# Moving weight conversion, small turning copies and filter loads between VectorE, ScalarE and GpSimd at the start of a kernel for a Fourier filter and a two-layer network

## The chip, the cores and the metric

One NeuronCore of one Trainium2 chip. The metric is device time in microseconds (us) of one execution. Executions of one kernel in one set of rounds lie within 0.33% of each other, and every ratio compares a kernel with runs of the kernel before from the same rounds on the same chip. In the lines of the profile PE is TensorE, PEld its weight loads, DVE VectorE, ACT ScalarE, POOL GpSimd and SP SyncE; a `q` behind the name marks what the engine's queue does besides computing, such as issuing a transfer. The DMA share is the busy share of the 16 DMA engines.

## The reference, cut to what matters

```python
# x: (8, 3008, 256) fp32; filt_r, filt_i: (1505, 256) fp32
X = np.fft.rfft(x, axis=1)
y = np.fft.irfft(X * (filt_r + 1j * filt_i)[None], n=3008, axis=1).astype(np.float32)
# w_in: (256, 2048), w_out: (2048, 256); they arrive as float64
h = y.reshape(8 * 3008, 256) @ w_in
out = ((h - np.tanh(h)) @ w_out).astype(np.float32)
```

The kernel does the transforms as matrix products in two steps (3008 = 47 x 64) through scratch tensors in DRAM, with the filter product between them, and the two large products by a scheme that takes seven block products in place of eight, which needs sums of weight blocks. The weights are doubles, so they are first made fp32 by integer operations on their two 32-bit words.

Words used below. A *piece* is 128x512 doubles (512 KB in DRAM); two pieces make a *quarter*, and there are eight quarters, four of `w_in` and four of `w_out`. The *first stage* is the forward transform of batch 0. The *middle stage* is 16 *steps*; a step is one product `pz`, two filter products on VectorE (`uv`, `zs`), the inverse product `pe`, its copy and its store. Two steps make a *step group*, for which the filter rows are loaded and the matrix `gx` is made ("turned"). The *passage* is what follows up to the main loop. A *unit* is a turn of the main loop, of which there are 192 in all: 14 up products, the shrink, 14 down products. Everything but batch 0's transforms lies in the main loop.

## The kernel before

One piece is converted like this; VectorE and ScalarE share the work, and ScalarE's two steps stand in its queue among its PSUM copies:

```python
def converted(tiles, src, dsts, queue):
    t = tiles("raw", I64, n); queue.dma_start(t, src)                       # cut
    yield
    V.tensor_scalar(out=it, in0=hi, scalar1=0xFFFFF, ..., op0=ALU.bitwise_and)
    ACT.activation(ft, it, AF.Identity, bias=1.0, scale=2.0 ** -20)
    V.tensor_scalar(out=pt, in0=hi, scalar1=20, scalar2=0x7FF, ...)
    ACT.activation(pt, pt, AF.Relu, bias=exp_b)
    V.tensor_scalar(out=st, in0=hi, scalar1=-2 ** 31, ..., op0=ALU.bitwise_and)
    V.scalar_tensor_tensor(out=ft, in0=lo, scalar=2.0 ** -52, in1=ft, ...)
    yield
    V.tensor_scalar_min(pt, pt, 255.0)
    V.scalar_tensor_tensor(out=pt, in0=pt, scalar=23, in1=st, ...)
    for cols, dst, sign in dsts:
        V.scalar_tensor_tensor(out=dst, in0=f, scalar=sign, in1=p, op0=ALU.mult, op1=ALU.mult)
    yield
# after the second piece of a quarter: four sums of 128x256 blocks, G.tensor_sub
```

`V` is VectorE, `ACT` ScalarE, `G` GpSimd. The middle stage and its helpers:

```python
def turned(g3, t):
    ACT.copy(t[0:RP], g3[IM:IM + RP])
    ACT.mul(t[IM:IM + RP], g3[0:RP], -1.0)

def back0():
    ...                                          # two products with mats, two with gx -> pe
    e1 = tr.tile([RP2, 2, DM], F32, tag="e1", bufs=2, name="e1")
    ACT.copy(e1, pe[0:RP2])
    ACT.dma_start(<scratch>, e1)

ws = weights(tiles0, range(5), 2)                # quarters 0 to 4, from the first stage on
for j in range(NK // 2):                         # 16 steps
    c = j // 2
    if j % 2 == 0 and c + 1 < NK // 4:
        a2[c + 1] = load_a2(0, c + 1, False)     # read-back of the first stage
        if c + 2 < NK // 4:
            mats[c + 2] = load_slots(c + 2, pro)
            fts[c + 2] = filters_of(c + 2)       # filter rows, 6 loads issued by GpSimd
    ...                                          # pz, then back0() of the step before
    V.tensor_mul(uv, pz, ft[:, 0])
    V.tensor_mul(zs, pz, ft[:, 1])
    next(ws, None)                               # a half of a piece
    if j % 2 and c + 1 < NK // 4:
        double_filters(fts[c + 1], c + 1)        # two ScalarE copies
        turned(mats[c + 1][1], gx[(c + 1) % 2])
back0(); load_e2(...)
for _ in range(EARLY):                           # EARLY = 3 forward products of the next batches
    next(fs)
```

In the main loop three quarters are left (`weights(tiles1, range(5, 8), 2)`, advanced at k = 0, 2, 4 of a unit), and the filter rows are copied once more for the later batches by small transfers of SyncE's queue.

## Time and profile before

| | us |
|---|---|
| time, median of 3 runs | 2882.33 (2880.47 to 2883.72) |
| same, beside the changed kernel, 6 runs | 2881.78 (2878.38 to 2883.72) |
| first middle product / first filter product | 43.0 / 45.2 |
| last result product ends | 106.6 |
| main loop's first unit starts | 123.4 |
| units 0 to 7 | 138.7 |
| from unit 8 to the end | 2617.2 |

The prediction shows the lines that this rests on. The table is read from the start of each unit's second product and from the first and last records of the step products. The first four rows of times lie in stretches that the change touches; the last, 91% of the time, has the same instructions in both kernels.

### The profile page before, as it was taken

Reading aid. Unit: us, or ns where it says so; the run is one execution under the profiler, and the core shown is the slowest. Engines: PE = TensorE matmul, PEld = TensorE weight load, DVE = VectorE, ACT = ScalarE, POOL = GpSimd, SP = SyncE. Lnnn points to the kernel's source line nnn. Section 1 sums busy time; section 2 is a strip of 40 time slices with the busy share of each in tenths; the row PEclk is TensorE's granted clock in tenths of the full one; section 3 lists DMA queues with packets and bytes.
Section 4 is the critical chain, followed back from the end, with each engine's and each line's share of the span. In section 5 each row is a group of like instructions: output and inputs, shape, how many; then the busy total and the mean of one; then the engine's idle time right before and its main releaser. Section 6 shows DMA issues by size and latency. Waiting matters only on the chain.

```text
span 2879.3 us, 36469 instructions
## 1 busy us (share of the span) xinstructions
PE 2748.1 (95%) x12474; PEld 2278.9 (79%) x12474; DVE 1989.3 (69%) x2214; ACT 1872.2 (65%) x2460; POOL 1743.4 (61%) x1382
## 2 busy tenths in 40 slices
PE   5789999999999999999999999999999999999996
PEld 3467777888878787888877888888888888888885
DVE  4675666766776677766677777766777777777765
ACT  3555666666767676666666676666666676666663
POOL 4345777544677767645576777655476666555544
PEclk7889999999999999999999999999999999999998
DMA  9644443232233332222323233112233222110100
GB/s 270 180 150 116 114 110 91 62 93 81 70 76 84 76 75 53 57 81 83 87 71 75 68 78 81 36 45 67 51 75 81 53 55 56 24 28 16 26 11 16
DMA packets 328061, 217.46 MB, mean 76 GB/s; under 512 B 229085, under 2 KB 280405, under 8 KB 327674
## 3 DMA queue, kind: packets, MB, share of 16 engines
q1 hardware_dynamic: 273176, 160.50, 23.6%
q10 hardware_dynamic: 52738, 51.33, 5.9%
q0 software_dynamic: 1952, 3.22, 0.5%
q8 instruction: 100, 1.64, 0.2%
q14 instruction: 95, 0.78, 0.1%
HBM read 138.81 MB, written 79.17 MB: 76 GB/s over the span
## 4 chain that ended last, share of the span: by engine, by line
PE 69%; DVE 9%; ACT 8%; POOL 5%; issue 4%; DMA 3%; SPq 1%; ACTq 0%; DVEq 0%; POOLq 0%
PE o L590 27%; PE x L483 18%; PE z L483 8%; PE y L483 5%; PE pe L364 3%; PE pu L447 3%; DVE h L544 3%; PE pz L383 3%; ACT y L539 2%; PE pf L304 2%; ACT y L540 1%; POOL t L465 1%; ACT u L489 1%; DVE uv L398 1%; DVE h L519 1%
## 5 line engine op out<-in xcount | busy, mean ns | idle before, releaser
L590 PE MATMUL o<-t,wd 128*128 128x256 f32 (+2 forms) x3072 | 777.9, 376 | 1.8 <-POOL t L464 1.3
L544 DVE TENSOR_TENSOR h<-h,y 128x1024 f32<-128x1024 f32 (+2 forms) x384 | 589.7, 1536 | 256.1 <-ACT y L540 255.9
L462 POOL TENSOR_TENSOR t<-h 128x512 f32<-128x512 f32 (+2 forms) x192 | 240.1, 1250 | 767.5 <-DVE h L548 582.3
L590 PEld LDWEIGHTS o<-t,wd 128*128 128x128 f32 x3072 | 582.0, 191 | 74.4 <-POOL t L464 1.9
L483 PE MATMUL x<-tu,wu 128*128 128x256 f32 (+2 forms) x2304 | 592.2, 380 | 16.5 <-ACT u L489 15.5
L590 PE MATMUL o<-h,wd 128*128 128x256 f32 (+2 forms) x2304 | 581.6, 375 | 0.2 <-DVE h L548 0.2
L548 DVE SCALAR_TENSOR_TENSOR h<-sq,h 128x1024 f32<-128x1024 f32 (+2 forms) x384 | 566.6, 1476 | 20.8 <-ACT y L539 0.5
L483 PEld LDWEIGHTS x<-tu,wu 128*128 128x128 f32 x2304 | 430.2, 191 | 157.2 <-issue 73.2
L590 PEld LDWEIGHTS o<-h,wd 128*128 128x128 f32 x2304 | 431.3, 190 | 70.8 <-issue 18.5
L545 ACT ACTIVATE sq<-y,near_b 128x1024 f32<-128x1024 f32 (+2 forms) x384 | 435.4, 1134 | 5.8 <-DVE h L548 1.1
L539 ACT ACTIVATE y<-h 128x1024 f32<-128x1024 f32 (+2 forms) x384 | 400.0, 1042 | 14.8 <-ACT e L367 6.8
L489 ACT COPY s<-x 128x512 f32<-128x512 f32 (+2 forms) x192 | 110.7, 577 | 458.2 <-PE x L483 449.6
L540 ACT ACTIVATE y<-y 128x1024 f32<-128x1024 f32 (+2 forms) x384 | 399.3, 1040 | 12.2
L465 POOL TENSOR_TENSOR t<-t,h 128x512 f32<-128x512 f32 (+2 forms) x192 | 306.7, 1597 | 0.0
L489 ACT COPY u<-x 128x512 f32<-128x512 f32 (+2 forms) x384 | 219.2, 571 | 73.0 <-PE x L483 35.5
L399 POOL TENSOR_TENSOR zs<-zs,ft 128x512 f32<-128x512 f32 x112 | 166.3, 1485 | 142.3 <-ACT zs L397 142.2
L463 POOL TENSOR_TENSOR t<-h,t 128x512 f32<-128x512 f32 (+2 forms) x192 | 241.6, 1258 | 15.0
L464 POOL TENSOR_TENSOR t<-h 128x512 f32<-128x512 f32 (+2 forms) x192 | 249.5, 1300 | 0.0
L400 POOL TENSOR_TENSOR uv<-uv,zs 128x512 f32<-128x512 f32 x112 | 211.3, 1887 | 16.0 <-DVE uv L398 7.8
L483 PE MATMUL x<-ut,wu 128*128 128x256 f32 (+2 forms) x768 | 200.0, 383 | 12.2 <-DVE h L519 10.7
L483 PE MATMUL z<-tu,wu 128*128 128x256 f32 (+2 forms) x768 | 195.4, 377 | 0.5 <-DVE h L525 0.5
L483 PE MATMUL z<-ut,wu 128*128 128x256 f32 (+2 forms) x768 | 194.8, 376 | 0.0
(113 smaller groups left out, 3236.6 us busy)
## 6 DMA issues: line engine op xcount, KB each, us to landing
a<-ct SPq DMA_DIRECT2D x64, 384.0 KB
ct<-e ACTq DMA_DIRECT2D x128, 192.0 KB
ft<-filt SPq DMA_DIRECT2D x96, 256.0 KB
out_dram<-ot SPq DMA_DIRECT2D x1408, 16.0 KB
ct<-a ACTq DMA_DIRECT2D x80, 256.0 KB
x_sb<-in_x_dram SPq DMA_DIRECT2D x69, 256.0 KB
e<-ct SPq DMA_DIRECT2D x33, 512.0 KB
fg<-fg SPq DMA_DIRECT2D x40, 392.0 KB
```

The lines of the kernel that those rows point to most:

```text
L462: G.tensor_sub(t[0], b[0][1], b[0][0])
L463: G.tensor_sub(t[1], b[1][1], t[0])
L464: G.tensor_sub(t[2], b[1][1], b[0][1])
L465: G.tensor_sub(t[3], t[1], b[1][0])
L483: nc.tensor.matmul(bank[:, k], wu[:, q - 1, (2 * u + k) * 128:(2 * u + k + 1) * 128], rhs[q - 1], start=(first and k == 0), stop=True, ski ...
L489: ACT.copy(t, X)
L539: ACT.activation(y[k], ht[k], AF.Arctan, scale=S)
L540: ACT.activation(y[k], y[k], AF.Square)
L544: V.tensor_mul(ht[k], ht[k], y[k])
L545: ACT.activation(sq[k], y[k], AF.Square, bias=near_b, scale=A)
L548: V.scalar_tensor_tensor(out=ht[k], in0=sq[k], scalar=K, in1=ht[k], op0=ALU.add, op1=ALU.mult)
L590: nc.tensor.matmul(product(q), wd[:, q - 1, (2 * u + k) * 128: (2 * u + k + 1) * 128], rhs[q - 1][:, k], start=(u == 0 and k == 0 and q == ...
```

## The change

Its intent: free ScalarE from weight conversion in the first stage, so that its PSUM copies follow TensorE; let VectorE do three quarters alone there and start the middle stage with fewer pieces left; take waits for buffers out of the middle steps (four result buffers instead of two, read-backs two groups ahead); take the passage's third forward product away; and leave two quarters instead of three to the main loop, in single steps instead of blocks, with the filter copies made few and large on GpSimd. The diff, cut to its core:

```diff
-EARLY = 3
+EARLY = 2
 def converted(...):
+        if alone:
+            V.tensor_scalar(out=ft, in0=it, scalar1=2.0 ** -20, scalar2=1.0, op0=ALU.mult, op1=ALU.add)
+            V.tensor_scalar(out=pt, in0=pt, scalar1=-896.0, scalar2=0.0, op0=ALU.add, op1=ALU.max)
+        else:
+            ACT.activation(ft, it, AF.Identity, bias=1.0, scale=2.0 ** -20)
+            ACT.activation(pt, pt, AF.Relu, bias=exp_b)
 ... (one manual_schedule region around everything, where there were two)
 def turned(g3, t):
-    ACT.copy(t[0:RP], g3[IM:IM + RP])
-    ACT.mul(t[IM:IM + RP], g3[0:RP], -1.0)
+    G.tensor_copy(t[0:RP], g3[IM:IM + RP])
+    G.tensor_scalar_mul(t[IM:IM + RP], g3[0:RP], -1.0)
-ws = weights(tiles0, range(5), 2)
+ws = weights_alone(tiles0, range(3))             # first stage, all of it ahead of the steps
+ws = weights(tiles0, range(3, 6), 2)             # middle stage, a piece finished one call later
-    e1 = tr.tile([RP2, 2, DM], F32, tag="e1", bufs=2, name="e1")
+    e1 = e1s[0:RP2, j % 4]
-        a2[c + 1] = load_a2(0, c + 1, False)
+        if c + 2 < NK // 4:
+            a2[c + 2] = load_a2(0, c + 2, False, ("a2", "ft")[c % 2])
 ... (main loop)
-    for c in range(NK // 4):
-        filters_of(c, filt_d)                    # 52 copies on SyncE
+    for v, row, m, i, n, src in filter_rows(0, NK):
+        G.dma_start(<filt_d>, src)               # 10 copies on GpSimd
-late = weights(tiles1, range(5, 8), 2)
+late = weights_slow(tiles1, range(6, 8))
-    if k in (0, 2, 4):
-        next(late, None)
-    elif U > 0:
-        next(copies, None)
+    next(late, None)
+    if U > 0 and k in (1, 3):
+        next(copies, None)
```

## The prediction

> **What bounds the kernel now.** I read the page first, then busy time by stretch, then the chain of waits of the first 125 us, then the waits. The page's slices of 72 us each show TensorE busy from the third slice to the end, and the DMA engines busy only at the start:
>
> ```profile
> PE   5789999999999999999999999999999999999996
> ...
> DMA  9644443232233332222323233112233222110100
> ```
>
> I compared the instruction order of both kernels on every engine. Apart from names they are the same from about the eighth unit of the main loop on (3175 of 3332 listed rows on PE, 2666 of 2862 on DVE), so only the time before that can change. A unit is a quarter of a group of four rows: 14 up products, the shrink, 14 down products; there are 192. From the start of each unit's second product I cut the beginning in four: first stage (forward transforms of batch 0, 0 to 43), middle stage (16 steps, to 107), passage to the main loop (to 123.4), units 0 to 7 (to 262.1). The view of busy time by stretch:
>
> ```profile
> 0.00:43.00 43.00, 14.63 (x26) 5.30 (x27) 12.05 (x26) 14.59 (x24) 18.56 (x33) 0.79 0.95 280
> 43.00:107.00 64.00, 52.87 (x194) 36.01 (x195) 47.92 (x90) 38.34 (x57) 33.94 (x56) 0.88 0.86 219
> 107.00:123.40 16.40, 8.99 (x26) 5.74 (x25) 0.83 (x1) 3.51 (x6) 1.44 (x3) 0.70 0.50 150
> 123.40:262.10 138.70, 118.92 (x469) 91.27 (x468) 97.01 (x124) 80.83 (x108) 53.98 (x51) 0.91 0.47 141
> 262.10:2879.00 2616.90, 2552.65 (x11763) 2140.56 (x11762) 1831.48 (x1975) 1734.92 (x2265) 1635.45 (x1243) 1.00 0.27 65
> ```
>
> Columns: stretch, length, PE, PEld, DVE, ACT, POOL busy, granted clock, DMA share, GB/s. The last row, 91% of the time, has PE at 98% and does not change. The 262 us before it hold the whole prize. The first stage is full on DMA (0.95), the middle stage nearly so (0.86); neither is full on any engine. The chain of waits there:
>
> ```profile
> 5.59 15.56 DMA raw<-in_moe_w_in_dram
> ...
> 21.80 0.63 ACT conv L205
> ...
> 58.71 4.96 DMA filt<-in_filt_i_dram
> 63.67 0.53 ACT filt L840
> ...
> 110.93 3.30 DMA x_sb<-in_x_dram
> ...
> 114.36 2.06 PE pf L304 x2
> ```
>
> First, ScalarE's half of a weight conversion stands ahead of PSUM copies in its queue and waits for weights that land at 21.15. Then the middle stage waits for filter rows. Then the first unit waits for an input tile queued behind a load that waits. The waits of 0 to 120 us (total, times, longest):
>
> ```profile
> ACT e L901 <- DMA ct<-e: 11.4, 5, 5.5
> ...
> DVE uv L922 <- ACT filt L839: 6.7, 3, 3.7
> ```
>
> The waits of SyncE's queue in the same stretch:
>
> ```profile
> SPq L417 <- DMA ct<-e: 19.6, 2, 11.0
> ```
>
> The waits of 123 to 262 us, where PE stands for a ScalarE copy that frees its bank and for input tiles:
>
> ```profile
> PE x L483 <- ACT u L489: 12.4, 5, 3.8
> ...
> PE pf L304 <- DMA x_sb<-in_x_dram: 6.9, 3, 4.2
> ```
>
> [...] three queues run and the share is 0.95. [...] the copies at 22.94 wait behind the conversion at 21.80. [...] Here single-source conversion steps start 0.34 us apart, two-tensor ones 0.61 to 0.73. [...] the three writes of a converted piece (L222) take 0.83 us alone and 3.92 us at 152.85 and at 192.27, in the combining sums of GpSimd.
>
> **The change part by part.**
>
> First stage. Before, two loads of late weights (1.05 MB) belong to the second region and yet stand sixth in SyncE's order, at 15.15; one region puts them after the first tiles of the main loop. That takes 1.05 MB at 280 GB/s, 3.7 us, out of a full stage. ScalarE loses its conversions, so its PSUM copies follow PE, which had all inputs but PSUM space at 19.4. Now the last copy is at 33.46, the stores issue to 35.1, the read-back issues at 38.31 and the first middle product starts at 43.02. I expect that product at 35 to 37. But six pieces, not three, stand on VectorE ahead of its first middle product, without help. One piece: three masks 1.02, two more single-source steps 0.68, then 0.61, 0.46, 0.73, 0.68: 4.2 us. Six from about 20.5 are 25 us, with 2 to 3 us for slowing by GpSimd's sums: about 48, where the first filter product now is at 45.16. So the 7 us do not reach VectorE; it starts about 3 us later.
>
> Middle stage. VectorE has 16 x 2 products at 0.60, 19.2 us, and six pieces at about 3.7, 22: 41 us, now 47.9 busy (seven pieces). Four result buffers instead of two take away "ACT e <- DMA ct<-e" (11.4 us; two waits, 5.5 and 3.5, stand ahead of the doubling of filters). Four a2 buffers load read-backs two steps ahead. ScalarE loses 8 x 1.03 us of turning, which GpSimd takes. A conversion is now finished one call later, so VectorE doesn't stand for ScalarE. If VectorE starts at 48, works 41 and waits 10 of the present 16, it ends at 99, now 104. By DMA: 219 GB/s x 64 us is 14.0 MB, plus the 1.05 MB moved here is 15 MB; from 36, at 246 GB/s (the rate of 40 to 80 us), that is 61 us: 97. Both say the stage ends at 99 to 100 instead of 107. Gain 7 us.
>
> Passage. EARLY = 2 takes away the third forward product, whose input stands behind a SyncE wait of 11 us and costs PE 6.05 us just ahead of the first unit. The path that stays is last store, second part of the tile, its products, two copies: about 12 us for 16.4. Gain 4 us.
>
> Units 0 to 7. Four late pieces for six: 2 x 6.3 us less VectorE time (a piece averages 6.3 us here: 2.8, 4.1, 3.6, 5.2, 3.0, 6.4 and 12.6 us over the six are 37.7). They are cut in five calls per unit, not run as blocks between the additions that free PSUM. 60 filter copies leave SyncE's queue for 10 large ones on GpSimd's, so input tiles no longer stand behind them (6.9 us of PE waits, of which I take 5). One more forward product costs 0.9. PE has 118.9 us of work at clock 0.91; 19.8 us are idle. I take 10 us of idle away, and 5 to 6 us of busy time because a steadier PE was granted more in this trace (1.00 in the stretches without holes, 0.72 in the one with most). 138.7 becomes about 123.5. Gain 15 us.
>
> Sum: 7 + 4 + 15 = 26 us, so 2882.3 - 26 = 2856 us.
>
> **The rivals.**
> 1. DMA is the bound of everything up to the main loop, and the order doesn't matter. For: 0.95, 0.86, and the same bytes but for their place. Against: in slices of 20 us the share falls to 0.76 (80 to 100) and 0.56 (100 to 120). Then the beginning gives at most 3 us, units 15: about 2864.
> 2. The conversions on VectorE become a new wait: six pieces in a row delay the middle stage, and GpSimd's sums of quarter 2 stand ahead of the filter rows of step group 2, which now are issued near 51 and land near 60 by a latency of 7 to 8 us. [...] Against: group 2 starts only at 63.66 today. If it holds, the beginning loses 3 to 5 us: about 2870.
> 3. PE fills the first units wholly and the start is DMA-tight at 0.98: 262 us x the idle I see allows 10 + 5 us at the start and 25 in the units: about 2840. Against: unit 1 has no down products, and the shrink's chain bounds it.
> 4. The large filter copies on GpSimd delay its combining sums (t), which three of the four down groups need. A GpSimd issue takes 0.54 us with 24, 28 or 64 runs alike, so I expect 10 x about 1 us off the path; if a copy of 496 runs costs several us each, 10 us of the gain go: 2866.
>
> **Range and chances.** The steps add to 26 us with 7 (start) and 7 (units) of doubt, and the rivals span 2840 to 2870. Eight in ten: 2838 to 2873. Over 2% needs 58 us of 262, more than PE idle and DMA slack I can name (about 40): 0.04. Slower by 2%: 0.01. Within: 0.95.
>
> **What would show it.** Right: first middle product before 38, first filter product near 48; last result copy near 98; first unit near 112; units 0 to 7 in 120 to 127 us; from unit 8 on 2617 us as before. Wrong: the middle stage still ending after 104 (rival 1 or 2: DMA share 0.95 says 1, gaps on DVE after the sums say 2); units 1 to 4 still over 18 us with VectorE full; a GpSimd issue over 2 us (rival 4); or the late part changing by more than 5 us, which would break the premise.

## The result, and the profile after

The changed kernel takes 2871.68 us (median of 6, 2866.68 to 2872.49) against 2881.78 us. The ratio is 0.9963, 95% interval 0.995 to 0.9975. A ratio here is the mean time of one kernel's runs over that of the other's runs of the same rounds, so it is not quite the ratio of the medians quoted. So the gain is 10 to 11 us, where 26 were predicted. It is clear of the noise and inside the stated range, but by the 2% rule the verdict is "same".

Where it came from needs more than one trace of each kernel, because single traces of one kernel differ in the table below by 0.4 us (first middle product) to 5.6 us (from unit 8 on). There are three of each (the two first profiles, and the runs `after_again`, `after_b`, `before_b`, `before_c` below):

| us, three traces and their mean | before | after | difference | predicted |
|---|---|---|---|---|
| first middle product starts | 43.0, 43.0, 42.6: 42.9 | 41.8, 42.2, 41.7: 41.9 | -1.0 | 35 to 37, so -6 to -8 |
| first filter product starts | 45.2, 45.2, 44.7: 45.0 | 52.1, 51.8, 51.7: 51.9 | +6.9 | +3 |
| last result product ends | 106.6, 108.8, 105.3: 106.9 | 115.0, 113.6, 113.9: 114.1 | +7.2 | -7 |
| passage (from there to the first unit) | 16.8, 16.6, 16.2: 16.5 | 12.7, 13.5, 13.6: 13.3 | -3.2 | -4 |
| units 0 to 7 | 138.7, 136.7, 134.0: 136.5 | 120.4, 119.1, 119.1: 119.5 | -16.9 | -15 |
| from unit 8 on | 2617.2, 2621.8, 2621.6: 2620.2 | 2616.3, 2621.9, 2621.6: 2619.9 | -0.3 | 0 |

The last four rows add up to -13.2 us in the traces; the timed difference is 10.7 (0.0037 of 2881.8), and single executions of either kernel spread over some 5 us. The gains of the passage and of units 0 to 7 came as forecast; the time up to the last result product, forecast to shrink by 7, grew by 7.

Busy time by stretch of the changed kernel, cut at the same events as the five lines of the kernel before (columns as there: stretch, length, PE, PEld, DVE, ACT, POOL busy with counts, granted clock, DMA share, GB/s):

```profile
0.00:41.80 41.80, 13.66 (x26) 4.96 (x27) 19.84 (x44) 10.06 (x16) 20.78 (x34) 0.83 0.91 258
41.80:114.80 73.00, 54.32 (x192) 38.58 (x193) 56.21 (x103) 30.17 (x41) 52.04 (x75) 0.77 0.82 210
114.80:127.70 12.90, 7.56 (x26) 5.60 (x25) 0.82 (x1) 2.92 (x5) 1.50 (x3) 0.69 0.82 244
127.70:248.10 120.40, 112.85 (x472) 88.00 (x471) 81.87 (x106) 78.87 (x105) 58.85 (x56) 0.96 0.52 155
248.10:2864.40 2616.30, 2552.98 (x11763) 2138.55 (x11761) 1828.85 (x1975) 1734.85 (x2265) 1637.03 (x1243) 1.00 0.26 65
```

Read row by row. First: ScalarE's work fell from 14.6 to 10.1 us as intended, the DMA rate fell from 280 to 258 GB/s, and the stretch is only 1.2 us shorter. Second: ScalarE fell from 38.3 to 30.2, VectorE rose from 47.9 to 56.2 and GpSimd from 33.9 to 52.0, and the stretch grew by 9 us. Fourth: TensorE is 94% busy where it was 86%; its idle time fell from 19.8 to 7.5 us, its busy time from 118.9 to 112.9 at a granted clock of 0.96 instead of 0.91. Fifth: the same work.

The waits of 0 to 125 us (total, times, longest), which answer to the two of the kernel before that the prediction shows:

```profile
ACT e1s L951 <- PE pe L948: 44.7, 10, 19.7
...
DVE uv L972 <- ACT filt L878: 10.4, 5, 5.5
...
PEld pe L948 <- POOL gx L888: 6.3, 1, 6.3
...
PE pe L948 <- POOL gx L888: 5.9, 1, 5.9
```

The wait of ScalarE's result copies for their stores (11.4 us before) is gone, as forecast. The wait of VectorE for doubled filters grew from 6.7 to 10.4. And a wait stands here that the kernel before had only in shares of 1 us: the inverse product stands 5.9 us for `gx`, now made by GpSimd. The chain of waits passes through it:

```profile
97.76 0.73 POOL wd L260
...
99.37 1.15 POOL wd L262
100.52 0.86 POOL wd L263
101.44 0.85 POOL gx L887
102.37 1.25 POOL gx L888
103.66 1.17 PE pe L948 x2
```

The timeline of GpSimd just before (start, length, engine, line, operation; in brackets the idle time and what ended it) shows why `gx` came so late:

```profile
88.37 0.60 POOL L874 DMA_DIRECT2D filt<-in_filt_r_dram  x1
88.96 0.55 POOL L874 DMA_DIRECT2D filt<-in_filt_i_dram  x1
91.23 0.58 POOL L874 DMA_DIRECT2D filt<-in_filt_r_dram  x1 [1.71 <-DMA filt<-in_filt_r_dram]
93.30 0.54 POOL L874 DMA_DIRECT2D filt<-in_filt_i_dram  x1 [1.49 <-DMA filt<-in_filt_i_dram]
```

GpSimd's instructions stand in this trace in the order of the program: ten issues for the filter rows of the last step group (steps 14 and 15), two of them waiting for transfers, then the four sums of a quarter of `w_out`, and only then the turning for the group before (steps 12 and 13): 15 us from 88.4 to 103.6, of which the turning itself is 2. The effect on the steps: up to the filter products of step 12 (96.4 us, against 95.9 before) the changed kernel had made up nearly all of its late start; step 14 then begins at 108.8 instead of 101.9.

In units 0 to 7 TensorE's wait for a ScalarE copy that frees its bank has shrunk from 12.4 us, and a line for input tiles, 6.9 us before, is no longer there:

```profile
PE x L547 <- ACT u L553: 7.1, 4, 4.9
```

### The profile page after: what moved, and what is told of

Same layout as the page of the kernel before. It is cut to its first block, busy times and chain, and to the rows that moved or that the text cites.

```text
span 2864.4 us, 36448 instructions
## 1 busy us (share of the span) xinstructions
PE 2741.4 (96%) x12474; PEld 2275.7 (79%) x12474; DVE 1987.6 (69%) x2226; ACT 1856.9 (65%) x2432; POOL 1770.2 (62%) x1408
## 4 chain that ended last, share of the span: by engine, by line
PE 71%; DVE 9%; ACT 8%; POOL 5%; issue 4%; DMA 2%; ACTq 0%; SPq 0%; DVEq 0%; POOLq 0%
PE o L654 28%; PE x L547 18%; PE z L547 8%; PE y L547 5%; PE pe L411 3%; PE pu L511 3%; PE pz L430 3%; DVE h L608 3%; ACT y L603 2%; PE pf L351 2%; ACT y L604 1%; POOL t L529 1%; ACT u L553 1%; DVE uv L445 1%; DVE h L583 1%
## 5 line engine op out<-in xcount | busy, mean ns | idle before, releaser
L547 PE MATMUL x<-tu,wu 128*128 128x256 f32 (+2 forms) x2304 | 589.0, 378 | 11.1 <-ACT u L553 10.1
L654 PEld LDWEIGHTS o<-h,wd 128*128 128x128 f32 x2304 | 430.8, 190 | 71.1 <-issue 18.3
L603 ACT ACTIVATE y<-h 128x1024 f32<-128x1024 f32 (+2 forms) x384 | 400.0, 1042 | 15.1 <-ACT e L414 7.5
L527 POOL TENSOR_TENSOR t<-h,t 128x512 f32<-128x512 f32 (+2 forms) x192 | 241.2, 1256 | 15.1
L563 DVE TENSOR_TENSOR h<-y,s 128x512 f32<-128x512 f32 (+2 forms) x192 | 130.3, 678 | 94.9 <-PE y L547 86.9
L547 PE MATMUL y<-ut,wu 128*128 128x256 f32 (+2 forms) x768 | 194.6, 376 | 0.0
```

What stands on the lines that cost most here:

```text
L527: G.tensor_sub(t[1], b[1][1], t[0])
L547: nc.tensor.matmul(bank[:, k], wu[:, q - 1, (2 * u + k) * 128:(2 * u + k + 1) * 128], rhs[q - 1], start=(first and k == 0), stop=True, ski ...
L603: ACT.activation(y[k], ht[k], AF.Arctan, scale=S)
L654: nc.tensor.matmul(product(q), wd[:, q - 1, (2 * u + k) * 128: (2 * u + k + 1) * 128], rhs[q - 1][:, k], start=(u == 0 and k == 0 and q == ...
```

## The experiments

All edits are to the changed kernel unless another is named. Times are medians of 4 or 5 runs (single runs in part D), ratios against the kernel before. "First unit" and "last product" are the start of the main loop's first unit and the end of the last result product in the profiled execution.

### A. The turning, and the middle stage

**after_again**: the changed kernel once more.

> The changed kernel once more, as a control for its own spread. Expected: ratio to before 0.995 to 0.998 again. Its beginning should show the same parts as in the first trace: first filter product near 52, a wait of about 6 us of PE for the turned matrices of GpSimd near 98 to 104, first unit near 127.7, units 0 to 7 in about 120 us, 2616 us from unit 8 on. If the first unit starts later than 130 in this trace, the spread of the changed kernel's times (2867 to 2872) lies in the beginning.

2870.68 us, 0.9963 [0.9949, 0.9976]. The result stands.

**t_act**: the turning back on ScalarE.

```diff
-    G.tensor_copy(t[0:RP], g3[IM:IM + RP])
-    G.tensor_scalar_mul(t[IM:IM + RP], g3[0:RP], -1.0)
+    ACT.copy(t[0:RP], g3[IM:IM + RP])
+    ACT.mul(t[IM:IM + RP], g3[0:RP], -1.0)
```

> The changed kernel with the turning of the matrices back on ScalarE. Theory (GpSimd's queue is the new wait: turning stands behind filter row issues, their waits, and sums): the 5.9 us wait of PE for gx goes, the filter rows are issued earlier, the middle stage ends 5 to 8 us sooner and the first unit starts at 120 to 123; total 5 to 8 us under the changed kernel, ratio to before 0.993 to 0.995. Rival (the stage's DMA bytes set its end): the wait moves to the filter rows or read-backs of the last group, the first unit stays at 126 or later, ratio 0.996.

2868.27 us, 0.9946 [0.9933, 0.996]; last product 112.3, first unit 125.5, 2 us sooner than the changed kernel's mean. A part of the loss only, and in the time not resolved from the changed kernel (0.9963 [0.9949, 0.9976]). TensorE's longest wait for `gx` in this trace is 0.6 us, so taking that wait away by this road is not enough: ScalarE is busy 19.4 us in 75 to 107 us where it was 13.6.

**t_first**: the turning stays on GpSimd, but is issued half a group sooner, ahead of the filter rows of the next group and of the sums.

```diff
-    (at odd j)  double_filters(fts[c + 1], c + 1); turned(mats[c + 1][1], gx[(c + 1) % 2])
+    (at even j, after back0)  turned(mats[c + 1][1], gx[(c + 1) % 2]); fts[c + 2] = filters_of(c + 2)
+    (at odd j)  double_filters(fts[c + 1], c + 1)
```

> The changed kernel with turning still on GpSimd, but issued ahead of the filter rows of the group after next, so that no sum and no filter issue stands between. It tells the place in the queue from the work. Theory of the queue: the gx wait of 5.9 us goes, gain 3 to 6 us on the changed kernel (ratio 0.994 to 0.996). If turning on GpSimd costs by its work or by slowing VectorE, this is no better than the changed kernel (0.9963).

2860.72 us, 0.9927 [0.9913, 0.994]: 10 us better than the changed kernel, intervals apart. GpSimd's timeline of this kernel for the same turning, now ahead of the last filter rows:

```profile
90.98 0.50 POOL L887 COPY gx<-fg 48x384 f32<-48x384 f32 x1 [2.43 <-DMA fg<-fg]
91.56 1.19 POOL L888 TENSOR_SCALAR gx<-fg 48x384 f32<-48x384 f32 x1
...
93.23 0.60 POOL L874 DMA_DIRECT2D filt<-in_filt_r_dram  x1
```

The long wait for `gx` is gone; its longest left in this trace is 0.9 us. Last product 110.0, first unit 124.0, where the changed kernel has 114.1 and 127.4. So the order in GpSimd's queue was a cost of the change, and about the whole loss against the kernel before (123.4). Its trace accounts for 3.4 us at the first unit, not for all 10 that the timing shows; the profiled execution was the slowest of its five (2866.14). What the other 6 are is not found; the part from unit 8 on took 2619.6 us in this trace, and it varies by 5 us from trace to trace in kernels that are alike there (part D).

That only brings the beginning back to where it was; the forecast wanted it 11 us sooner. The next runs ask what holds it then.

**no_loads** (wrong): t_first, with pieces 6 to 11 converted from the raw tiles of pieces 3 to 5 instead of being loaded, so 3.1 MB fewer are moved in the middle stage and VectorE's work stays.

```diff
+    (pieces 6 to 11)  t = loaded[3 + len(loaded) % 3]     # no transfer
```

> On the kernel t_first, pieces 6 to 11 of the weights (the six converted during the middle stage) are converted from pieces 3 to 5, already in SBUF, so six loads of 0.52 MB are not made; all instructions of the engines stay. The result is wrong on purpose. Theory (the middle stage's end is set by DMA bytes): 3.1 MB at the 229 GB/s of 75 to 107 us are 13.7 us, so the first unit starts 9 to 14 us sooner than in t_first (124.0), at 110 to 115. Rival (engine queues set it, VectorE's row of conversions and GpSimd's queue): under 4 us, first unit at 120 or later.

Last product 106.4, first unit 119.1: 4.9 us sooner than t_first. Time 2860.07, 0.993 [0.9915, 0.9945], no different from t_first's. The 4.9 us lie between the theory (9 to 14) and its rival (under 4). Busy time in 75 to 107 us, of t_first and of no_loads:

```profile
75.00:107.00 32.00, 24.34 (x97) 17.07 (x98) 26.61 (x51) 16.33 (x22) 26.37 (x40) 0.95 0.90 229
```

```profile
75.00:107.00 32.00, 27.31 (x114) 18.60 (x115) 28.22 (x52) 18.27 (x26) 29.13 (x42) 1.00 0.59 168
```

The DMA share falls from 0.90 to 0.59, and VectorE and GpSimd are then busy 28.2 and 29.1 of 32 us. The bytes were a limit, and another stands right behind it.

**alone2**: t_first, with two quarters converted by VectorE alone before the steps instead of three, and the third with ScalarE's help among the steps.

```diff
-ws = weights_alone(tiles0, range(3))
+ws = weights_alone(tiles0, range(2))
-ws = weights(tiles0, range(3, 6), 2)
+ws = weights(tiles0, range(2, 6), 2)
+    (at j % 4 == 3)  next(ws, None)              # one more call, so that it ends in time
```

> On t_first, only two quarters instead of three are converted by VectorE ahead of the middle stage, the third with the rest during it (four extra calls). Theory (DMA sets the stage's end, so when VectorE starts doesn't matter): first filter product at 42 to 45 instead of 51.9, yet the first unit still at 122 to 126, total within 3 us of t_first (2860.7). Rival (the six pieces in a row cost the stage what they delay it): first unit 4 to 8 us sooner, ratio to before 0.990 to 0.9915.

The first filter product comes at 41.3 instead of 51.9, and the last product still ends at 108.4; 2860.64 us, 0.993 [0.9917, 0.9944], the same as t_first. Ten us of earlier start bought less than two at the end: the six pieces in a row ahead of the first step cost little, because the same work only moved behind it. Two things in this trace are easily overlooked. The first middle product comes at 39.1, sooner than in any trace of the changed kernel (taken up in the part on the prediction's first stage). And in 42 to 75 us the DMA engines are full, with a share of 1.05 where t_first has 0.88:

```profile
42.00:75.00 33.00, 24.91 (x99) 17.57 (x97) 24.83 (x46) 15.94 (x23) 27.16 (x40) 0.93 1.05 263
```

**alone2_no_loads** (wrong): alone2 without the loads of pieces 6 to 11.

> alone2 and no_loads together: VectorE starts the middle stage at 41 instead of 52, and six of the weights' loads are not made. The result is wrong on purpose. Theory (two limits side by side: bytes hold the stage to 108 to 110, VectorE's work after a start at 52 holds it to 106; each alone gave 2 to 5 us): with both lifted the last product of the stage ends at 94 to 99 and the first unit starts at 106 to 112, 8 us or more before either alone (119.1, 120.8). Rival (a third limit, the chain of filter rows, ScalarE's doubling and VectorE): first unit stays at 116 or later.

Last product 108.2, first unit 119.8; 2859.04 us, 0.9927 [0.9912, 0.9942]. With the DMA share at 0.46 in 75 to 107 us the stage ends where it did; the expectation's rival came true, not its theory.

**alone2_light** and **alone2_light_no_loads** (both wrong): alone2 with pieces 6 to 11 not converted, their places filled with zeros by VectorE (ScalarE's two steps per piece go too); the first still loads them, the second doesn't. With the two runs above that makes all four combinations.

```diff
+    if 6 < len(loaded) <= 12:                    # pieces 6 to 11
+        for cols, dst, sign in dsts:
+            V.memset(dst, 0.0)
+        return
```

> Kernel alone2 (two quarters converted by VectorE alone, GpSimd turning ahead of its filter rows), with pieces 6 to 11 still loaded but not converted: their places are filled with zeros by two or three memsets on VectorE (wrong on purpose). About 6 x 5 us of VectorE's work in the middle stage goes, the bytes stay. If VectorE's conversions are the limit of the middle stage: last result product at 98 to 102 instead of 108.4, first unit near 111 to 115 instead of 120.8. If the DMA engines' bytes are: 106 to 109 and 119 to 121, no change, DMA share 0.9 in 75 to 107 us. If neither alone (both side by side, each hiding the other): 104 to 107. Rest unchanged but for the zeros; read the first unit's start, not the total.

> As alone2_light, and pieces 6 to 11 not loaded either (wrong on purpose): both the bytes (3.1 MB) and VectorE's conversions of the middle stage go. If these two are the whole limit: last result product at 88 to 95, first unit at 100 to 107. If the chain of the 16 steps itself (filter rows, GpSimd's queue, ScalarE's copies and result stores) is a third limit close behind: last result product still at 100 to 106, with VectorE busy under 20 of 32 us in 75 to 107 and DMA share under 0.6.

| last product ends / first unit starts, us | six pieces converted | not converted |
|---|---|---|
| six pieces loaded | 108.4 / 120.8 | 105.2 / 118.0 |
| not loaded | 108.2 / 119.8 | 100.8 / 113.2 |

Busy time in 75 to 107 us, of alone2, alone2_no_loads, alone2_light and alone2_light_no_loads in this order:

```profile
75.00:107.00 32.00, 23.61 (x83) 16.46 (x84) 29.14 (x54) 16.51 (x23) 23.84 (x36) 0.84 0.74 209
```

```profile
75.00:107.00 32.00, 26.04 (x89) 17.79 (x88) 28.91 (x54) 16.38 (x23) 26.23 (x36) 0.79 0.46 122
```

```profile
75.00:107.00 32.00, 24.98 (x92) 16.70 (x92) 12.56 (x28) 13.77 (x18) 22.28 (x35) 0.84 0.80 213
```

```profile
75.00:107.00 32.00, 24.49 (x90) 16.70 (x90) 10.79 (x26) 11.77 (x16) 21.10 (x34) 0.89 0.57 161
```

Taking away the bytes alone gives 0.2 us at the last product, the conversions alone 3.2, both 7.6. These are single traces, and three traces of one kernel differ by 1.4 us (changed) to 3.5 us (before) at this event. What is firm is that both together give far more than either. Which of the two comes first is less sure; the traces suggest VectorE's conversions (29 of 32 us busy), with the bytes close behind them (without the conversions, VectorE waits 24.5 us in 42 to 107 us for filters that ScalarE doubles, and ScalarE in turn 13.0 for the filter rows to land), and the 99 to 100 us of the forecast are all but reached only with both gone. The expectation for the second run, 88 to 95, was too hopeful: with VectorE busy for a third of 75 to 107 us and the DMA engines for 0.57 of it, the steps end at 100.8, within the 100 to 106 of that expectation's alternative. That this is the chain of the 16 steps itself is not shown: in 42 to 75 us the DMA share is 1.01 to 1.05 in all four kernels, so the transfers that are left fill that stretch. The zeros are no help in the late part: 2619.3 and 2616.6 us from unit 8 on, within the spread seen above. The totals, 2860.59 (0.9925 [0.9906, 0.9945]) and 2853.37 us (0.9905 [0.9888, 0.9921]), against 2860.64 for alone2 and 2859.04 for alone2_no_loads, say the same: one gone gives nothing that is resolved, both gone 7 us (its interval just touches alone2's).

**two_bufs**: two result buffers instead of four.

```diff
-e1 = e1s[0:RP2, j % 4]
+e1 = tr.tile([RP2, 2, DM], F32, tag="e1", bufs=2, name="e1")
```

> The changed kernel with two result buffers in the middle stage, as before, instead of four. The prediction counted their removal of waits (11.4 us of ScalarE for stores) among what shortens the stage. If those waits lie on the path, the first unit starts 3 to 6 us later than 127.4 and the ratio is 0.998 to 0.9995. Theory now (the stage is held by bytes, VectorE and GpSimd's queue): within 2 us, ratio 0.9955 to 0.997.

2869.33 us, 0.9961 [0.9947, 0.9975], as with four. The wait itself came back in the waits of 0 to 125 us:

```profile
ACT e L950 <- DMA ct<-e: 13.7, 6, 4.5
```

13.7 us of waiting that cost nothing: last product 114.1, first unit 127.7, against means of 114.1 and 127.4. The prediction counted the removal of this wait (11.4 us before) for the middle stage. It lies beside the real limits.

### B. The first stage and the passage

**before_one**: the kernel before with one scheduling region instead of two, which moves only the two late weight loads out of the first stage.

```diff
-    with tc.tile_pool(name="tr", bufs=2) as tr:
+    with tc.tile_pool(name="tr", bufs=2) as tr, tc.manual_schedule():
```

> The kernel before with one region in program order and nothing else; only the two hoisted loads of late weights (1.05 MB) move, from SyncE's sixth row to behind the first tile of the main loop. The prediction's step: 3.7 us out of the first stage. If so the first middle product comes at 39 to 40 instead of 43.0 and the first unit 2 to 4 us sooner; ratio 0.9985 to 0.9993. Rival (the first stage ends by its stores, and what the loads give back is taken by the loads' new place in front of the second tile): first middle product after 41, first unit within 1.5 us of 123.4, ratio 0.9995 to 1.0005.

2879.37 us, 0.9998 [0.9984, 1.0012]; first middle product at 43.8 (before 42.6 to 43.0), first unit at 124.7. The 1.05 MB that leave a stage with a DMA share of 0.95 give nothing.

**early3**: EARLY = 3 again.

> The changed kernel with three forward products ahead of the main loop, as before. The prediction gave 4 us to the passage, by the third product's wait for its input tile. If that is right the time from the last product of the middle stage to the first unit is 15 to 17 us instead of 12.7 to 13.5, ratio 0.997 to 0.998. Rival (the tiles are now loaded ahead of the waiting load, so the third product costs only its 0.9 us, or nothing since unit 0 to 7 lose one): under 14 us, ratio 0.996 to 0.9968.

The passage takes 15.1 us instead of 13.3, the first unit starts at 128.8; 2871.97 us, 0.9964 [0.9951, 0.9978], no different from the changed kernel. The part of the passage that belongs to EARLY is 2 us in the trace and is not resolved in the time.

### C. The main loop's first units

**late_blocks**: the late pieces as blocks at k = 0, 2, 4, as before. **copies_sync**: the filter rows copied by 52 transfers on SyncE, as before. **units_old**: both.

```diff
-late = weights_slow(tiles1, range(6, 8))
+late = weights(tiles1, range(6, 8), 2)           # late_blocks, units_old
-    next(late, None)
+    if k in (0, 2, 4): next(late, None)          # late_blocks, units_old
-    G.dma_start(<filt_d>, src)                   # 10
+    nc.sync.dma_start(<filt_d>, src)             # copies_sync, units_old: 52, up to four filters each
```

> The changed kernel with the late pieces in blocks at three calls a unit, the filter copies on GpSimd as changed. Together with units_old (units 0 to 7 in 132.9 us against 120) it parts the loop's gain in two. Theory: the blocks stand ahead of the additions that free PSUM, and cost 5 to 9 of the 13 us: units 0 to 7 in 125 to 129 us, ratio 0.998 to 0.9995. Rival (the copies on SyncE are the whole of it): under 122 us, ratio 0.996 to 0.997.

> The changed kernel with the filter copies in 60 pieces on SyncE's queue, the late pieces in single steps as changed. Theory: input tiles stand behind the copies, 4 to 8 us of the 13: units 0 to 7 in 124 to 128 us, ratio 0.998 to 0.999. Rival (the copies cost nothing on either queue): under 122 us, ratio 0.996 to 0.997.

> The changed kernel with the old main loop: late pieces converted in blocks at three calls a unit, and the filter copies in 60 pieces on SyncE's queue. It tells what the loop's part is worth. Theory (the gain of 18 us in units 0 to 7 comes from these two, the rest of the change costs 4 us): units 0 to 7 take 130 to 138 us again and the total is 2880 to 2888, ratio 0.999 to 1.002. Rival (the gain comes from having two quarters left instead of three): units 0 to 7 stay under 126 us and the ratio stays under 0.998.

| | time, us | ratio [95%] | units 0 to 7, us | TensorE waits there for input tiles, us |
|---|---|---|---|---|
| late_blocks | 2875.03 | 0.9991 [0.9978, 1.0005] | 128.7 | 6.9 |
| copies_sync | 2871.23 | 0.9975 [0.9961, 0.9988] | 124.2 | 3.5 |
| units_old | 2884.70 | 1.0011 [0.9997, 1.0024] | 132.9 | 12.6 |
| changed kernel (after_again; units: mean of three traces) | 2870.68 | 0.9963 [0.9949, 0.9976] | 119.5 | none |

With both undone, units 0 to 7 take 13.3 us longer and the kernel is no faster than the kernel before. Alone they cost 9.2 and 4.7. The 3.6 us that are left to the 136.5 of the kernel before remain for what units_old does not undo, mainly two quarters instead of three to convert; no run shows that part by itself.

In all three the waits for input tiles grow along with the units. How a block causes one is seen in the longest unit of late_blocks (24.3 us; 16.9 with single steps). TensorE, then SyncE's queue:

```profile
154.45 1.03 PE L547 MATMUL y<-ut,wu 128*128 128x256 f32 x4
161.18 2.04 PE L351 MATMUL pf<-x_sb,wf_sb 128*128 128x512 f32 x2 [5.71 <-DMA x_sb<-in_x_dram]
```

```profile
154.79 0.38 SPq L197 DMA_DIRECT2D raw<-in_moe_w_out_dram  x1
155.26 1.96 SPq L1006 DMA_DIRECT2D ct<-zero  x4
157.34 1.05 SPq L330 DMA_DIRECT2D x_sb<-in_x_dram  x2
```

The load of the next piece (L197) stands at the head of SyncE's queue until VectorE has read the old piece for the last time, and the input tile (L330) stands behind it. The longest such waits in units 0 to 7, in late_blocks and then in the changed kernel:

```profile
SPq L197 <- DVE ft L219: 16.0, 1, 16.0
```

```profile
SPq L197 <- DVE pt L221: 6.3, 1, 6.3
```

The kernel before has the same wait four times, 30.7 us in total, and its filter copies in the same queue wait 25.5 us for other transfers. So both parts of the change act through SyncE's queue. The profile of late_blocks lists no wait of TensorE for one of VectorE's additions in these units.

The ten large copies on GpSimd are cheap to issue, each 0.5 to 0.7 us:

```profile
195.81 0.74 POOL L1019 DMA_DIRECT2D filt<-in_filt_r_dram  x1
196.55 0.71 POOL L1019 DMA_DIRECT2D filt<-in_filt_i_dram  x1
```

### D. The late part

**before_b**, **before_c**, **after_b**: one more look at each kernel, for the late part's own spread.

> The kernel before, unchanged, for a second trace of its late part (from unit 8 on). If the late part varies by itself from trace to trace (as the traces of the changed kernel and its variants do: 2616 to 2622 us, all of it in the last 380 us): this trace and the next lie anywhere in 2616 to 2622. If the change lengthens the late part: 2617 again. First unit at 123 to 124, units 0 to 7 at 136 to 139.

> The kernel before once more, with the same expectations: a spread of 2616 to 2622 us in the late part if it varies by itself, 2617 if the change lengthens it.

> The changed kernel once more: late part 2616 to 2622 us. First unit at 127 to 128, units 0 to 7 at 119 to 121.

Late parts of 2621.8, 2621.6 and 2621.6 us. The late part varies by 5 us from trace to trace in both kernels; with 2617.2 and 2616.3 in the two first profiles those happened to be a fair pair. One trace of the kernel before had also flattered the prediction's units: 138.7 us where the mean is 136.5.

## Why the prediction was right or wrong

**Late part unchanged: right**, -0.3 us between means.

**Units 0 to 7: right in size, in part by another path.** 16.9 us where 15 were forecast (18.3 between the first two profiles). The two terms measured as told: 12.2 us of idle time (10 forecast) and 6.1 of busy time (5 to 6). The busy time went through the clock: 118.92 us at 0.91 and 112.85 at 0.96 are the same product, 108. The undoing runs assign 13.3 us to the single steps and the filter copies together. But the prediction charged the blocks to "the additions that free PSUM" and the waits for input tiles to the filter copies alone; late_blocks shows 6.9 us of waits for input tiles from the blocks, and none for the additions. And of the "60 filter copies" only 52 left SyncE's queue; the eight transfers beside them that fill rows with zeros stay. Rival 4 is refuted, with 0.74 us at most for the issue of a large copy in place of several.

**Passage: right**, 3.2 us of 4; early3 gives 1.8 of them to the third product.

**First stage: wrong in both terms.** "I expect that product at 35 to 37" rested on the premise that ScalarE, without conversions, follows TensorE. It lost its conversions, but its queue also issues the stores, and those stand in it. ScalarE's queue in the changed kernel, two issues of two stores each and the copies behind them:

```profile
21.67 2.45 ACTq L862 DMA_DIRECT2D ct<-a  x2
24.24 1.07 ACT L858 COPY a<-pf 128x512 f32<-128x512 f32 x2 [2.85 <-DMA raw<-in_moe_w_in_dram]
...
27.82 2.93 ACTq L862 DMA_DIRECT2D ct<-a  x2
30.86 0.86 ACT L858 COPY a<-pf 128x512 f32<-128x512 f32 x2 [3.08 <-DMA raw<-in_moe_w_in_dram]
```

One issue takes 0.58 us, and two take 1.25 where nothing is in their way (33.32 in the same list); here they take 2.45 and 2.93, because the second of the two waits until a weight tile of SyncE's queue has landed, as the brackets say. In the packed trace it waits on the semaphore that this load signals (signalled at 23.52 and 30.14, the second issues start at 23.54 and 30.17), though it uses none of its data. The last copy starts at 32.92, 0.5 us sooner than before, and the read-back then takes 4.4 us to land. alone2 and its three variants, which have one weight load fewer ahead of the read-back, show what was to be had: there the pairs after 21 us take 1.25 to 1.53 us, the last pair is issued at 31.0 to 31.5 instead of 33.0 to 33.3, and the first middle product comes at 38.9 to 39.7 instead of 41.7 to 42.2. How much of that is the waits and how much the bytes, no run separates. Taking 1.05 MB of late weights out of the stage of the kernel before gave nothing (before_one), so the 3.7 us of "1.05 MB at 280 GB/s" were no saving there; in the changed kernel 22 GB/s less were moved instead. The "first filter product near 48" came at 52.1: VectorE started at 21.8 for 20.5; one free piece took 4.15 us as forecast (24.9 for six); but slowing was 4.7 us for "2 to 3", and 0.6 was a wait for the sixth piece's load.

The slowing shows in the two timelines, VectorE's and then GpSimd's, of the third piece:

```profile
30.06 0.42 DVE L204 TENSOR_SCALAR conv<-raw 128x512 int32<-128x512 int32 x1
30.39 0.95 DVE L205 TENSOR_SCALAR conv<-raw 128x512 int32<-128x512 int32 x1
31.26 0.94 DVE L207 TENSOR_SCALAR conv<-raw 128x512 int32<-128x512 int32 x1
32.13 0.94 DVE L211 TENSOR_SCALAR conv<-conv 128x512 f32<-128x512 int32 x1
32.99 0.94 DVE L213 TENSOR_SCALAR conv<-conv 128x512 int32<-128x512 int32 x1
```

```profile
30.30 0.76 POOL L260 TENSOR_TENSOR wu<-wu 128x256 f32<-128x256 f32 x1 [18.16 <-DVE wu L230]
31.14 0.78 POOL L261 TENSOR_TENSOR wu<-wu 128x256 f32<-128x256 f32 x1
32.00 0.79 POOL L262 TENSOR_TENSOR wu<-wu 128x256 f32<-128x256 f32 x1
32.75 0.90 POOL L263 TENSOR_TENSOR wu<-wu 128x256 f32<-128x256 f32 x1
```

Each of the four sums starts, and the VectorE step beside it ends only after that sum has: 0.94 us for 0.42. So 0.52 us are lost beside each sum. That the sums are the cause is read from these two lists; no run isolates it.

**Middle stage: wrong, and this is the step that failed.** "If VectorE starts at 48, works 41 and waits 10 of the present 16, it ends at 99": in the changed kernel it starts at 52.1, is busy 46.6 of the 60.6 us to the end of its last product and idle for 14.1 (the view of busy time cut to that stretch):

```profile
52.07:112.70 60.63, 48.47 (x175) 34.45 (x176) 46.56 (x85) 29.59 (x40) 49.46 (x71) 0.81 0.81 204
```

So the sum of 99 was short by 4.1 at the start, 5.6 of work and 4.1 of waits. VectorE's work, forecast to fall by 6.9 us, fell by 1.4. At the 0.60 us of the forecast the 32 filter products take 19.2, so the six pieces took 27.4, or 4.6 each for "about 3.7". That 3.7 did not fit the kernel before either: its seven pieces took 28.7 of the 47.9 us, or 4.1 each. So about 2.4 us of the missing work were mis-sized from the start, and some 3 came with the change; GpSimd is busy 49.5 us in that stretch against 31.2 of 59.3 in the kernel before, and in the first stage each of the single-source VectorE steps beside its sums took 0.5 us more (0.94 for 0.42; for the middle stage this is inferred). The "present 16" of waits was misread too: it is VectorE's idle time of 43 to 107, while from its first to its last product the kernel before is idle for 11.4 (59.3 less 47.9). The waits of the changed kernel: the one for `gx` is new, because work that was 8 x 1.03 us on ScalarE went into GpSimd's program behind issues that wait for transfers and behind the sums (13.1 us of them, 88.4 to 101.4). The prediction said only "which GpSimd takes". t_first shows its worth: 3 to 4 us at the first unit, 10 us in the time. Four result buffers, counted as a relief, gave nothing (two_bufs). What else makes up the 14.1 us is not taken apart.

The second working, "By DMA ... 97", agreed with the first and made it look safe; but it assumed that the stage runs at its best rate throughout. The four combinations show that neither bytes nor VectorE alone set the end: lifting one leaves the other, and 100.8 is what both together give.

**Of the rivals, the second held.** It said that conversions on VectorE become a new wait, that GpSimd's sums stand ahead of step work, that the beginning loses 3 to 5 us, and 2870. Measured: 4.0 us lost at the first unit and 2871.7. Its detail was off: what stood behind the sums were not the filter rows of group 2 but the turning for the last group but one. It was set aside because "group 2 starts only at 63.66 today", a look at one group of eight; the queue was worst near the end.

**What would have shown it wrong** was named well: the middle stage ended after 104, with a DMA share of 0.82 rather than 0.95, and the gap of 5.9 us on TensorE ends right behind the sums and the turning.

The versions t_first and alone2, at 2860.7 and 2860.6 us, beat both kernels and are correct; they are equal within the spread.

## What to carry to other kernels

When work moves to another engine, write down what stands ahead of it in that engine's program at the worst turn, waits included, not only how long it takes; here 13.1 us of GpSimd's issues, waits and sums stood ahead of 2.2 us of turning, and issuing it before the issues that wait was worth as much as the whole change (10 us each). A busy-time estimate for one engine and one for the DMA engines that agree do not confirm each other: where both limits lie side by side, removing one shows little (0.2 us for the bytes, 3.2 for the conversions, 7.6 for both). A stall is to be followed to the engine that matters: the blocks of conversion cost through the loads that stood behind them in SyncE's queue, not through the additions next to them (6.9 us of TensorE's waits for input tiles in late_blocks, none for the additions). And take several traces before pricing a stage to a few us.

## What the traces showed of single instructions

- Four 128x256 sums of GpSimd beside 128x512 single-source steps of VectorE (the third piece, 30.3 to 33.9 us): VectorE's steps took 0.94 to 0.95 us where they took 0.42 alone, 2.1 us in all; the sums took 0.76 to 0.90 us where 0.72 is the shortest seen, 0.35 us in all.
- The turning on 48x384 fp32: on GpSimd in the changed kernel the copy took 0.50 us at best and the multiplication by a constant 1.16 at best; the same two took 0.50 and 0.52 on ScalarE in the kernel before.
- The time of one instruction stream varies by itself: the part from unit 8 on, alike in both kernels, took 2616.3 to 2621.9 us in six traces.
